# Scores by four 64x64 matmuls side by side, in two bursts per batch, for batches 2 to 7

## The chip, the cores and the metric

The kernel runs on one core of one Trainium2 chip. A core has a matrix engine (TensorE, in the profile PE, its weight loads PEld), VectorE (DVE), ScalarE (ACT), GpSimd (POOL) and a queue engine (SyncE, SP), which work through their own instruction streams in order and wait for each other by semaphores. The metric is the device time of one execution in microseconds (us). Less is better.

## The reference

Sliding-window causal attention over 8 batches and 8 heads, followed by two dense layers with a gate between them:

```python
B, H, S, D = 8, 8, 576, 64                    # q, k, v: [B, H, S, D] float32
scores = q @ k.T / sqrt(D)                    # per batch and head
scores = where((0 <= i - j) & (i - j < 64), scores, -1e9)
attn = softmax(scores)                        # over the keys
x = (attn @ v).transpose(0, 2, 1, 3).reshape(B * S, H * D)     # 4608 x 512
h = x @ w_in                                  # w_in 512 x 2048
out = (h * cos(h)) @ w_out                    # w_out 2048 x 512, out 4608 x 512 float32
```

A query sees only itself and the 63 keys before it. So the 576 rows of a batch and head fall into 9 blocks of 64 queries, and block j needs the keys of blocks j - 1 and j alone (block 0 only its own 64).

## The kernel before, in words

**Units and groups.** Heads are taken in four pairs p. A unit (b, p, j) is the scores of one pair and one query block: 128 rows (64 queries of each of the two heads) by 128 keys. Up to four units make a group, which shares one PSUM bank and goes as one through the softmax: `g_scores` (TensorE), `g_max` (VectorE: mask, scale and row minimum of the negative, out of PSUM), `g_exp` (ScalarE, one exponential per unit), `g_inv` (VectorE reciprocal), `g_norm` (the product with it, on GpSimd, for one group of batch 2 on VectorE) and `g_trans` (a transposing DMA from the SP queue, which makes the weights wT). `CUTS` lists, batch by batch, which query blocks form the groups and in which order: batch 2 takes blocks 0 to 5 of all pairs first, batch 3 blocks 0 to 4, the others 0 to 3.

**Scores of batches 2 to 7.** q stands in SBUF in a padded form `qB`: for each pair and block a 128x128 tile with head 0's 64x64 in one corner, head 1's in the opposite one, and zeros (memsets `ms.0` to `ms.7` in the list `FIRST`) in the others. One 128x128 matmul per unit (line 303) then gives both heads' scores. q gets there by TensorE transposes (`tr_q`, line 219) and two half copies by VectorE (`put_block`), or, for the chunks counted in `TURNED`, by a transposing DMA (`turn_q`) and VectorE copies (`put_turned`). k is turned by transposing DMAs in six chunks (`turn_k`).

**Values and the dense layers.** 4608 rows make nine tiles mt of 512 rows (8 blocks each, while a batch has 9, so tile mt starts in batch mt - 1 and ends in batch mt for mt from 2 to 7). Per tile: `values` (line 384, attention times v, pair after pair, 16 matmuls each), `put_x` (copies to xT; the one of pair 2 by ScalarE), 64 matmuls h_ps (line 453) with a sine by ScalarE and a product by VectorE behind each four, and 64 matmuls out_ps (line 609).

**What sets the order.** Each engine's stream is written out by hand: up to tile 1 by the list `FIRST`, then by planned times. `at(time, step)` puts a step on a plan, `pump(time)` issues all that is due; one tile is T = 32 units of planned time, 16 for h_ps and 16 for out_ps. The scores of batch b are issued in tile b - 1 from planned time 14.6 on, a group after each few out_ps matmuls (`PACE`), each later step of a group by its lag (`LAGS`: 0.2, 1, 3, 3.2, 3.8). In the same tile GpSimd copies half of batch b's v rows to the other half of the partitions (`spread_v`, two copies at planned time 24 for batch 3 and 22.2 for later ones; for batch 2 a DMA does it at 10), and issues the loads. The values of tile b are planned at the end of tile b - 1. PSUM has eight banks: five named ones (O0, O1, X0, X1, S), which h_ps, out_ps and scores share, and three in a rotating pool `ps_t` (tag "t"), which the transposes of q and the values use.

**Batches 0 and 1** are scored by 64x64 matmuls, one per head, the two of a pair on opposite quarters of TensorE's array (line 309).

Of the kernel before, what the change touches and what calls it, by code (L numbers as in the profile page):

```python
# [10 lines left out]
def _safe_warn(msg, *a, **kw):  # L11
# [12 lines left out]
NU = 9  # L24
NC, NP = 6, 96
GF = 4
LAST = 384
PACE = 0.36
CUTS = (
# [6 lines left out]
)  # L36
# [39 lines left out]
def kernel(  # L76
# [28 lines left out]
    first_q = moe.tile([128, 2, d_model], F32, tag="out", name="qT", bufs=OUTS).rearrange("p a f -> p (a f)").bitcast(BF16)  # L105
    qtiles = [first_q[:, S * i:S * i + S] for i in range(PAIRS - 1)]
    qtiles.append(const.tile([128, S], BF16, name="qT3"))
    turned = const.tile([128, PAIRS, S], BF16, name="qT")
    qtiles += [turned[:, p] for p in range(PAIRS)]
    qsets = [const.tile([128, PAIRS, NU, 2, 64], BF16, name=f"qB{i}") for i in range(2)]  # L110
    qblocks = [qset[:, p] for qset in qsets for p in range(PAIRS)]
# [16 lines left out]
    S_BANKS = ("X1", "S", "X0")  # L128
# [146 lines left out]
    for b, cuts in enumerate(CUTS, 2):  # L275
        for cut in cuts:
            for p0 in range(0, PAIRS, 2):
                for of, lo, hi in cut:
                    groups += [[(b, p, j) for p in range(p, p + of) for j in range(lo, hi)] for p in range(p0, p0 + 2, of)]
    direct = set(range(n_first)) | {n_first + i for i in DIRECT}  # L280

    def g_scores(n, which):
        s_ps = bank((BANKS if n < n_listed else S_BANKS)[which], "s_ps")
# [12 lines left out]
        for u, (b, p, j) in enumerate(units):  # L296
            kt = st["kT", b, p]
            lo, chunks = max(64 * j - 64, 0), 2 if j else 1
            rhs = kt[:, lo:lo + 64 * chunks].rearrange("d (a t) -> d a t", a=chunks)
            if j and j % 2 == 0:  # L300
                rhs = rhs[:, ::-1, :]
            if b > 1:
                nc.tensor.matmul(out=s_ps[:, u, 0:64 * chunks].rearrange("p (a t) -> p a t", a=chunks),  # L303
                                 lhsT=qblocks[(b % 2) * PAIRS + p][:, j].rearrange("d h t -> d (h t)"), rhs=rhs,
                                 start=True, stop=True, skip_group_check=True)
                continue
            for h in range(2):
                d = slice(64 * h, 64 * h + 64)
                nc.tensor.matmul(out=s_ps[d, u, 0:64 * chunks].rearrange("p (a t) -> p a t", a=chunks),  # L309
                                 lhsT=qtiles[b * PAIRS + p][d, 64 * j:64 * j + 64], rhs=rhs[d], start=n >= n_first,  # L310
                                 stop=n >= n_first or u == len(units) - 1, skip_group_check=True)
# [3 lines left out]
    def g_max(n):  # L315
# [4 lines left out]
        else:  # L320
            s = att.tile([128, GF, 128], F32, tag="s", name="s", bufs=4)
            for u, (b, p, j) in enumerate(units):
# [7 lines left out]
    def g_exp(n):  # L330
# [3 lines left out]
        for u, (_, _, j) in enumerate(groups[n]):  # L334
# [5 lines left out]
    def g_inv(n):  # L340
        e, den = st["e", n]
        for u, (_, _, j) in enumerate(groups[n]):
# [13 lines left out]

    def g_trans(n):
# [10 lines left out]
        st.update({("wT", unit): wT[:, i] for i, unit in enumerate(groups[n])})  # L368

    def g_put(n, engine=None):  # L370
        wT, u = att.tile([128, GF, 128], BF16, tag="wT", name="wT", bufs=20), len(groups[n])
        copy(engine, wT[:, 0:u], st.pop(("tw", n))[:, 0:u])
        st.update({("wT", unit): wT[:, i] for i, unit in enumerate(groups[n])})


    def values(mt, p, lo=0, hi=TU):
# [3 lines left out]
        for i in range(lo, hi):  # L380
            b, j = divmod(mt * TU + i, NU)
            wT = st["wT", (b, p, j)]
            for h in range(2):
                nc.tensor.matmul(out=o_ps[64 * h:64 * h + 64, 64 * i:64 * i + 64],  # L384
                                 lhsT=vtiles[b % 2][:, max(j - 1, 0), 128 * p + 64 * h:128 * p + 64 * h + 64],
                                 rhs=wT[:, 64 * h:64 * h + 64], start=True, stop=True, skip_group_check=True)
# [9 lines left out]
    def values_half(a, g):  # L396
        st["o", a, g] = o_ps = ps_t.tile([128, 2, half], F32, tag="t", name="o_ps")
        for p in (0, 1):
            for i in range(GF):
                j = GF * g + i  # L400
                wT = st["wT", (0, 2 * a + p, j)]
                for h in range(2):
                    nc.tensor.matmul(out=o_ps[64 * h:64 * h + 64, p, 64 * i:64 * i + 64],
                                     lhsT=vtiles[0][:, max(j - 1, 0), 128 * (2 * a + p) + 64 * h:128 * (2 * a + p) + 64 * h + 64],
                                     rhs=wT[:, 64 * h:64 * h + 64], start=True, stop=True, skip_group_check=True)
# [81 lines left out]
    ready = {(0, p, j): 0 for p in range(PAIRS) for j in range(TU)}  # L487
    ready.update({unit: 0 for units in groups[:n_listed] for unit in units})
    n = n_listed
    for t in range(1, B - 1):  # L490
        last = max(i for i, units in enumerate(groups) if units[0][0] == t + 1)
        time = T * t + Q - 1.4
        for i in range(last + 1 - n):
            time += PACE * len(groups[n - 1]) if i else 0
            at(time, g_scores, n, i % 3)
            lags = LAGS[:2] + tuple(T * t + T - 0.79 - time + 0.01 * s for s in range(3)) if n == last else LAGS
# [3 lines left out]
            at(time + (4.6 if n in direct else lags[-1]), g_trans, n)  # L500
            if n in direct:
                at(time + 4.9, g_put, n)
            ready.update({unit: time + (5.9 if n in direct else 8.5) for unit in groups[n]})
            n += 1

    for b in range(2, B):
        t0 = T * (b - 1)
        for h in range(2):
            if b in TURNED:
                at(t0 + 0.6 + 0.5 * h, put_turned, b, h, 0, 3)  # L510
            if TURNED.get(b, 0) > 2:
                at(t0 + (11 + h if TURNED[b] == NC else 10 + 0.5 * h), put_turned, b, h, 3, TURNED[b] * NP // 64)
        for c in range(TURNED.get(b, 0)):
            at(t0 - T + (24.3 if b == 4 else 23.4 if c < 2 else 26.4) + 0.01 * c, turn_q, b, c)
        for p in range(PAIRS if TURNED.get(b) != NC else 0):
            t_q = t0 + (2 if b == 2 else 1) + (3.3 if b == 2 else 3.5) * p
            for lag, fn, *args in ((0, tr_q), (0.02, put_block, 0), (0.5, put_block, 1)):
                at(t_q + lag, fn, b, p, *args)
# [130 lines left out]
```

## Time and profile before

| | us |
|---|---|
| Time, median of 3 runs (lowest to highest) | 310.14 (308.4 to 311.36) |
| Profiled execution: span from first to last instruction | 306.3 |
| Profiled execution: its own time | the page gives the span alone |
| TensorE busy (matmuls) | 296.2 |
| ScalarE busy | 234.3 |
| VectorE busy | 228.5 |
| GpSimd busy | 192.5 |

Everything in the page and the trace counts from the span's start; between the span and the time of a run lie 3.8 us by the median. The busy time of an engine is an average over stages: h_ps and out_ps alternate, and the softmax runs beside out_ps. The chain of waits names, piece by piece in order of time, the work that ended last; the timeline names each instruction of one engine; DMA answers give the us from issue to landing.

### The profile page before, as it was taken

The numbers are of one execution on the slowest core, as the hardware profiler recorded it, in microseconds if no ns is written. First come the engines' busy times: TensorE is split into PE (matmuls) and PEld (weight loads), VectorE is DVE, ScalarE is ACT, GpSimd is POOL, SyncE is SP. The second block draws the span as 40 slices with busy tenths as digits, with TensorE's granted clock in tenths as the row PEclk, the third lists the DMA queues.
The fourth block names the chain that finished last, engine by engine and source line by source line (L and its number), as shares of the span: only waits on it lengthen the run. The fifth ranks groups of instructions, "written<-read, shape, count | busy, mean of one in ns | idle before, by whom it ended". The sixth has DMA issues, their size and how long they took to land.

```text
span 306.3 us, 7904 instructions
## 1 busy us (share of the span) xinstructions
PE 296.2 (97%) x2616; PEld 159.0 (52%) x2616; DVE 228.5 (75%) x908; ACT 234.3 (76%) x785; POOL 192.5 (63%) x228
## 2 busy tenths in 40 slices
PE   3889999999999999999999999999999999999996
PEld 2768844545555555445544555454545554454443
DVE  5999978599769976798579857986698668235801
ACT  5998799677997799779976997699879986116600
POOL 8998579995659669967998599959903930000000
PEclk9999999999999999999999999999999999999999
DMA  7999999999999995999999999999794643011011
GB/s 146 179 212 192 200 180 130 121 149 191 226 113 116 175 223 80 121 133 232 125 121 137 231 143 104 157 221 148 86 137 107 169 78 141 2 68 71 1 67 70
DMA packets 159945, 42.14 MB, mean 138 GB/s; under 512 B 148256, under 2 KB 155168, under 8 KB 159904
## 3 DMA queue, kind: packets, MB, share of 16 engines
q0 software_dynamic: 100192, 18.06, 80.1%
q1 hardware_dynamic: 59568, 23.38, 40.6%
q8 instruction: 20, 0.33, 0.4%
q14 instruction: 21, 0.17, 0.2%
q10 hardware_dynamic: 144, 0.20, 0.2%
HBM read 36.70 MB, written 9.44 MB: 151 GB/s over the span
## 4 chain that ended last, share of the span: by engine, by line
PE 90%; POOL 4%; DMA 2%; DVE 1%; ACT 1%; issue 1%; POOLq 0%; DVEq 0%; ACTq 0%
PE h_ps L453 35%; PE out_ps L609 35%; PE h_ps L417 5%; PE s_ps L303 4%; PE out_ps L436 4%; PE o_ps L384 3%; DMA k<-in_k_dram 2%; POOL w L353 2%; PE tq_ps L219 1%; POOL v L188 1%; PE out_ps L465 1%; PE s_ps L309 1%; PE tw_ps L364 1%; POOL w_in L204 1%; ACT e L336 1%
## 5 line engine op out<-in xcount | busy, mean ns | idle before, releaser
L609 PE MATMUL out_ps<-w_out,gT 128*128 128x512 bf16 x496 | 117.3, 379 | 0.0
L453 PE MATMUL h_ps<-xT,w_in 128*128 128x512 bf16 x512 | 115.3, 379 | 0.3
L595 ACT ACTIVATE sin<-h_ps 128x512 f32<-128x512 f32 x128 | 73.7, 598 | 32.7 <-PE h_ps L453 31.4
L598 DVE TENSOR_TENSOR gT<-h_ps,sin 128x512 bf16<-128x512 f32 x128 | 82.1, 685 | 21.9 <-ACT sin L595 21.2
L336 ACT ACTIVATE e<-s,negm 128x128 f32<-128x128 f32 (+1 forms) x256 | 97.1, 382 | 0.6 <-DVE negm L324 0.6
L353 POOL TENSOR_TENSOR w<-e,rden 128x512 bf16<-128x512 f32 (+1 forms) x74 | 70.0, 962 | 36.6 <-DVE rden L346 18.8
L453 PEld LDWEIGHTS <-w_in 128*128 128x128 bf16 x512 | 48.8, 98 | 54.7 <-issue 0.4
L609 PEld LDWEIGHTS <-gT 128*128 128x128 bf16 x496 | 45.9, 98 | 44.2
L324 DVE CUSTOM_DVE_ANT_0 s<-s_ps,mask 128x128 f32<-128x128 f32 (+1 forms) x256 | 56.4, 279 | 1.7 <-PE s_ps L309 0.9
L336 ACT ACTIVATION_READ_ACCUMULATOR e<-s,negm 128x1 f32 x256 | 48.3, 189 | 0.0
L182 POOL DMA_DIRECT2D q<-in_q_dram x36 | 28.3, 785 | 10.7 <-DMA q<-in_q_dram 4.0
L188 POOL DMA_DIRECT2D v<-in_v_dram x40 | 34.4, 878 | 0.3 <-issue 0.2
L182 POOL DMA_DIRECT2D k<-in_k_dram x36 | 28.2, 783 | 3.9 <-DMA k<-in_k_dram 1.2
L137 ACT COPY out_sb<-out_ps 128x512 f32<-128x512 f32 (+1 forms) x18 | 10.2, 566 | 24.5 <-PE out_ps L609 18.4
L346 DVE RECIPROCAL rden<-den 128x4 f32<-128x4 f32 (+1 forms) x79 | 13.1, 166 | 19.0 <-ACT e L336 18.6
L303 PEld LDWEIGHTS <-qB 128*128 128x128 bf16 x216 | 16.5, 98 | 14.2
L137 DVE CAST xT<-o_ps 128x512 bf16<-128x512 f32 x24 | 15.5, 677 | 10.1 <-PE o_ps L384 10.1
L137 DVE COPY out_sb<-out_ps 128x512 f32<-128x512 f32 x18 | 12.4, 690 | 13.2 <-PE out_ps L609 12.5
L324 DVE DVE_READ_ACCUMULATOR2_ANT negm<- 128x1 f32 x256 | 21.3, 83 | 0.0
L303 PE MATMUL s_ps<-kT,qB 128*128 128x128 bf16 (+1 forms) x216 | 21.2, 216 | 0.0
L137 POOL COPY v<-v 64x1536 bf16<-64x1536 bf16 (+3 forms) x12 | 18.8, 1570 | 0.3
L137 DVE COPY qB<-tq_ps 64x384 bf16<-64x384 bf16 (+1 forms) x40 | 15.6, 390 | 0.4
(70 smaller groups left out, 257.8 us busy)
## 6 DMA issues: line engine op xcount, KB each, us to landing
out_dram<-out_sb SPq DMA_DIRECT2D x16, 512.0 KB, 7.5
v<-in_v_dram POOLq DMA_DIRECT2D x32, 128.0 KB, 5.7
q<-in_q_dram POOLq DMA_DIRECT2D x36, 96.0 KB, 8.6
k<-in_k_dram POOLq DMA_DIRECT2D x36, 96.0 KB, 8.5
w_in<-in_moe_w_in_dram POOLq DMA_DIRECT2D x4, 512.0 KB, 8.7
w_out<-in_moe_w_out_dram POOLq DMA_DIRECT2D x4, 512.0 KB, 10.8
wT<-w SPq DMA_TRANSPOSE x68, 4.4
q<-in_q_dram POOLq DMA_DIRECT2D x7, 144.0 KB, 6.0
```

What stands on the lines that cost most here:

```text
L137: {"a": nc.scalar.copy, "p": nc.gpsimd.tensor_copy}.get(engine, nc.vector.tensor_copy)(out, in_)
L182: nc.gpsimd.dma_start(out=st[name, b][:, c].rearrange("p (h d) -> p h d", h=H), in_=src.rearrange("h p d -> p h d"))
L188: nc.gpsimd.dma_start(out=vt.rearrange("p (h d) -> p h d", h=H), in_=v[b, :, c * 128:c * 128 + n, :].rearrange("h p d -> p h d"))
L303: nc.tensor.matmul(out=s_ps[:, u, 0:64 * chunks].rearrange("p (a t) -> p a t", a=chunks), lhsT=qblocks[(b % 2) * PAIRS + p][:, j].rearrang ...
L324: nc.vector.tensor_tensor_reduce(out=s[:, u, c], in0=s_ps[:, u, c], in1=mask[:, 2 - j % 2 if j else 0, c], scale=-scale if b else -1.0, sc ...
L336: nc.scalar.activation(e[:, u, c], s[:, u, c], AF.Exp, bias=negm[:, u:u + 1], scale=1.0 if n < n_first else -1.0, accum_out=den[:, u:u + 1])
L353: (nc.gpsimd if engine == "p" else nc.vector).tensor_tensor(out=w[:, 0:u], in0=e[:, 0:u], op=ALU.mult, in1=rden[:, 0:u].unsqueeze(2).to_br ...
L417: nc.tensor.matmul(out=h_ps[:, half * e:half * e + half], lhsT=w_in_sb[:, ks, ff * 128:ff * 128 + 128], rhs=st["xT", 0][:, ks, half * g:ha ...
L453: nc.tensor.matmul(out=st["h", ff], lhsT=w_in_sb[:, ks, ff * 128:ff * 128 + 128], rhs=st["xT", mt][:, ks], start=start, stop=stop)
L595: nc.scalar.activation(sin, h_ps, AF.Sin, bias=math.pi / 2.0)
L598: nc.vector.tensor_tensor(out=gt[:, e], in0=h_ps, in1=sin, op=ALU.mult)
L609: nc.tensor.matmul(out=o_ps[e], lhsT=gT[ff // 2][:, ff % 2, ms * 128:ms * 128 + 128], rhs=w_out_sb[:, ff], start=ff == 0, stop=ff == n_ff - 1)
```

## The change

For batches 2 to 7 the padded q is given up. q is held once per pair (`qsets`, two buffers of 128 x 4 x 576, taken in turn by even and odd batches; batches 0 and 1 use them too); TensorE's transposes are copied out by one copy of all 128 partitions, and the turning DMA writes into it without a copy behind it. The memsets go.

The scores are taken in two bursts per batch, at planned times 14.6 (query blocks 0 to 3, four banks: X1 and three of the rotating pool) and 20.6 (blocks 4 to 8, five banks: S, X0, X1 and two of the pool). A group now holds two neighbouring blocks of all four pairs, for one head of each pair: its unit (b, a, j, h) is head h of pairs 2a and 2a + 1, on the two halves of the 128 rows. Two groups, one for each h, are filled together, so that four 64x64 matmuls in a row use the four quarters of the array, two into each of two banks. Block 8 forms a ninth group of the old kind. The later steps of group n of a batch are planned at 14.6 + 1.6 n and the same lags. `wT` is kept by head. Nine groups per batch take the place of ten to twelve; the `s` buffers go from four to six. Batches 0 and 1 are scored as before.

```diff
-PACE = 0.36
-CUTS = (
-    (((1, 0, 4), (2, 4, 6)), ((1, 6, 9),)),
-    (((1, 0, 3), (2, 3, 5)), ((1, 5, 9),)),
-    (((1, 0, 4),), ((1, 4, 7), (2, 7, 9))),
...
-)
+PACE = 1.6
+BURSTS = ((0, 4, ("X1", "t", "t", "t")), (4, 8, ("S", "X0", "X1", "t", "t")))
+BURST = (14.6, 20.6)
...
-    qsets = [const.tile([128, PAIRS, NU, 2, 64], BF16, name=f"qB{i}") for i in range(2)]
-    qblocks = [qset[:, p] for qset in qsets for p in range(PAIRS)]
+    qsets = [const.tile([128, PAIRS, S], BF16, name=f"qT{i}") for i in range(2)]
...
     def put_q(b, p, engine=None):
-        of, to = in_order(st.pop(("tq", b, p)), qtiles[b * PAIRS + p], b)
+        if b > 1:
+            lo = TURNED.get(b, 0) * NP
+            copy(engine, qsets[b % 2][:, p, lo:], st.pop(("tq", b, p))[:, lo:])
+            return
+        of, to = in_order(st.pop(("tq", b, p)), qsets[b][:, p], b)
...
-    def put_block(b, p, h):
-        d = slice(64 * h, 64 * h + 64)
-        lo = TURNED.get(b, 0) * NP // 64
-        copy("d", qblocks[(b % 2) * PAIRS + p][d, lo:, h], st["tq", b, p][d].rearrange("d (j t) -> d j t", j=NU)[:, lo:])
-
     def turn_q(b, c):
-        nc.sync.dma_start(out=turned[:, :, c * NP:c * NP + NP], in_=st["q", b][:, c], transpose=True)
-
-    def put_turned(b, h, lo, hi):
-        d = slice(64 * h, 64 * h + 64)
-        copy("d", qsets[b % 2][d, :, lo:hi, h], turned[d].rearrange("d a (j t) -> d a j t", j=NU)[:, :, lo:hi])
+        nc.sync.dma_start(out=qsets[b % 2][:, :, c * NP:c * NP + NP], in_=st["q", b][:, c], transpose=True)
...
-    for b, cuts in enumerate(CUTS, 2):
-        for cut in cuts:
-            for p0 in range(0, PAIRS, 2):
-                for of, lo, hi in cut:
-                    groups += [[(b, p, j) for p in range(p, p + of) for j in range(lo, hi)] for p in range(p0, p0 + 2, of)]
+    bursts = []
+    for b in range(2, B):
+        for lo, hi, banks in BURSTS:
+            bursts.append((b, len(groups), banks))
+            for j in range(lo, hi, 2):
+                groups += [[(b, a, j + e, h) for e in range(2) for a in range(2)] for h in range(2)]
+        groups.append([(b, p, NU - 1) for p in range(PAIRS)])
...
+    def burst_scores(n):
+        b, g0, banks = bursts[n]
+        for g, which in enumerate(banks, g0):
+            s_ps = ps_t.tile([128, MT], F32, tag="t", name="s_ps") if which == "t" else bank(which, "s_ps")
+            st["s", g] = s_ps.rearrange("p (u c) -> p u c", c=128)
+        for g in range(g0, g0 + len(banks), 2):
+            for u in range(GF):
+                for n in range(g, min(g + 2, g0 + len(banks))):
+                    _, p, j, *h = groups[n][u]
+                    for e in range(2):
+                        pe, he = (2 * p + e, h[0]) if h else (p, e)
+                        d = slice(64 * he, 64 * he + 64)
+                        rhs, chunks = keys(b, pe, j)
+                        to = st["s", n][64 * e:64 * e + 64, u, 0:64 * chunks]
+                        nc.tensor.matmul(out=to.rearrange("p (a t) -> p a t", a=chunks),
+                                         lhsT=qsets[b % 2][d, pe, 64 * j:64 * j + 64], rhs=rhs[d], start=True, stop=True,
+                                         skip_group_check=True)
...
-            if b > 1:
-                nc.tensor.matmul(out=s_ps[:, u, 0:64 * chunks].rearrange("p (a t) -> p a t", a=chunks),
-                                 lhsT=qblocks[(b % 2) * PAIRS + p][:, j].rearrange("d h t -> d (h t)"), rhs=rhs,
-                                 start=True, stop=True, skip_group_check=True)
-                continue
...
+    def put_wT(n, wT):
+        for i, (b, p, j, *h) in enumerate(groups[n]):
+            for e in range(2):
+                st["wT", (b, 2 * p + e, j, h[0]) if h else (b, p, j, e)] = wT[:, i, 64 * e:64 * e + 64]
...
-                                 rhs=wT[:, 64 * h:64 * h + 64], start=True, stop=True, skip_group_check=True)
+                                 rhs=st["wT", (b, p, j, h)], start=True, stop=True, skip_group_check=True)
...
+    for i, (b, g0, banks) in enumerate(bursts):
+        t = T * (b - 1)
+        at(t + BURST[i % 2], burst_scores, i)
+        for n in range(g0, g0 + len(banks)):
+            time = t + BURST[0] + PACE * (n - bursts[i - i % 2][1])
+            lags = LAGS[:2] + tuple(t + T - 0.79 - time + 0.01 * s for s in range(3)) if n == bursts[i | 1][1] + 4 else LAGS
             for lag, fn in zip(lags, (g_max, g_exp, g_inv)):
                 at(time + lag, fn, n)
             at(time + lags[3], g_norm, n, "d" if n == n_listed + 5 else "p")
-            at(time + (4.6 if n in direct else lags[-1]), g_trans, n)
...
+            at(time + lags[4], g_trans, n)
...
-    def clear_first(p, engine):
-        (nc.gpsimd if engine == "p" else nc.vector).memset(qblocks[p].rearrange("d j h t -> d (j h t)"), 0.0)
```

More of the change, by code (lines that the diff above doesn't have):

```diff
@@ L296, in g_scores @@
         for u, (b, p, j) in enumerate(units):
[L297 to L301, printed above, removed]
-            if b > 1:
-                nc.tensor.matmul(out=s_ps[:, u, 0:64 * chunks].rearrange("p (a t) -> p a t", a=chunks),
-                                 lhsT=qblocks[(b % 2) * PAIRS + p][:, j].rearrange("d h t -> d (h t)"), rhs=rhs,
-                                 start=True, stop=True, skip_group_check=True)
-                continue
+            rhs, chunks = keys(b, p, j)
             for h in range(2):
@@ L333, in g_exp @@
         den = att.tile([128, GF], F32, tag="den", name="den", bufs=8)
-        for u, (_, _, j) in enumerate(groups[n]):
+        for u, (_, _, j, *_) in enumerate(groups[n]):
             c = slice(0, 128 if j or n < n_first else 64)
@@ L341, in g_inv @@
         e, den = st["e", n]
-        for u, (_, _, j) in enumerate(groups[n]):
+        for u, (_, _, j, *_) in enumerate(groups[n]):
             if j == 0 and n >= n_first:
@@ L367, in g_trans @@
         nc.sync.dma_start(out=wT[:, 0:u], in_=w[:, 0:u].rearrange("p u c -> p (u c)"), transpose=True)
-        st.update({("wT", unit): wT[:, i] for i, unit in enumerate(groups[n])})
+        put_wT(n, wT)
     def g_put(n, engine=None):
@@ L372, in g_put @@
         copy(engine, wT[:, 0:u], st.pop(("tw", n))[:, 0:u])
-        st.update({("wT", unit): wT[:, i] for i, unit in enumerate(groups[n])})
+        put_wT(n, wT)
     def values(mt, p, lo=0, hi=TU):
```

47 lines of the change are left out of this document (12 added, 35 removed), and 13 rows, old and new, of tables (CUTS, FIRST).

## The prediction, made before the changed kernel had run

> **What bounds the kernel now.** I read the page's engine totals first, then the chain of waits, then the table by stage.
>
> ```profile
> PE 296.2 (97%) x2616; PEld 159.0 (52%) x2616; DVE 228.5 (75%) x908; ACT 234.3 (76%) x785; POOL 192.5 (63%) x228
> PE 90%; POOL 4%; DMA 2%; DVE 1%; ACT 1%; issue 1%; POOLq 0%; DVEq 0%; ACTq 0%
> core 0: us, PE busy (x) PEld busy (x) DVE busy (x) ACT busy (x) POOL busy (x), PEclk, DMA share, GB/s
> 135.88:152.76 16.88, 16.85 (x166) 9.09 (x162) 12.82 (x92) 16.81 (x78) 13.97 (x15) 1.00 1.55 179
> 152.76:167.40 14.64, 14.64 (x83) 7.06 (x83) 12.65 (x27) 10.27 (x17) 13.16 (x17) 1.00 1.93 124
> ```
>
> TensorE carries 90% of the chain at clock 1.00, so an edit is worth the TensorE time it removes, as long as no wait moves in. The two stretches are one period. In the second (h_ps) every other engine has slack. In the first (scores, out_ps, values) ScalarE is busy for 16.81 of 16.88 us: the weights of a batch come out at the pace of the exponentials, whatever TensorE does. The chain of waits of that stretch, when batch 4 is scored:
>
> ```profile
> 135.88 0.20 PE s_ps L303 x4
> 136.08 1.73 PE out_ps L609 x8
> ...
> 148.15 3.45 PE out_ps L609 x16
> 151.60 1.13 PE o_ps L384 x64
> 152.73 0.03 issue
> 152.76 2.75 PE h_ps L453 x12
> ```
>
> From 135.88 to 151.60 are 15.72 us. The 64 out_ps matmuls take 64 x 3.45/16 = 13.80, so the scores take 1.92 us a batch, 11.5 us in six batches. Nothing else stands there.
>
> **The change, part by part.** Scores. Per batch, 36 matmuls of 128x128 become 72 of 64x64: a burst of 32 and one of 40. Batch 1 of this kernel already runs 64x64 matmuls, two side by side:
>
> ```profile
> 40.04 0.48 PE s_ps L309 x14
> 40.53 1.83 PE out_ps L436 x8
> 42.36 0.34 PE s_ps L309 x8
> 37.14 0.57 PE tq_ps L216 x36
> ```
>
> Fourteen against eight are three more pairs, one of them 64 columns wide, for 0.14 us: 0.056 for a full pair, 0.028 for the short one, as much as one full-size score matmul. Eight in 0.34 leave 0.34 - 4 x 0.056 = 0.12 for leaving the shape, and out_ps behind a burst costs 1.83 where eight otherwise cost 1.73 (row at 136.08): 0.10 more. A burst has a fixed price of 0.22.
>
> What no row shows is four tiles at once. Below, a set of four cannot beat 0.056 (one pair); above, it costs 0.111 (two pairs in turn). The nearest rows say how fast small matmuls with their weight loads can follow: 36 in 0.57 are 0.016 each, 0.063 a set. I take 0.056, since two pairs on different quarters need what one pair needs, and keep 0.111 for the range. Burst one: 6 sets at 0.056, 2 short ones (row block 0 sees 64 keys) at 0.028, 0.22: 0.61. Burst two: 8 sets, 4 pairs for row block 8, 0.22: 0.89. Sum 1.50, 0.42 less per batch, 2.5 us in six.
>
> [...]
>
> Padding gone. Eight memsets, the doubled q copies and the copies out of the turned q leave VectorE, all in stretches where TensorE waits for other things or for nothing:
>
> ```profile
> L546 DVE MEMSET qB<- 128x576 uint32 x8 | 4.3, 538 | 0.6
> 14.51 4.09 POOL w L353 x4
> ```
>
> The start hangs on loads and then on GpSimd's four products at 14.51, so I credit 0. Should VectorE's freed time pull the first products forward, that is 0.1 at most: GpSimd issues loads until 14.31.
>
> ScalarE. Same 36 exponentials, starting behind the same table load, so their ends stay. With TensorE 0.42 ahead, xT's third part is what could be late next:
>
> ```profile
> 152.52 0.59 ACT L137 CAST xT<-o_ps 128x512 bf16<-128x512 f32 x1
> ```
>
> It is ready at 152.52 + 0.59 = 153.11. TensorE wants it after six h_ps matmuls, 152.76 + 1.30 = 154.06, then 153.64. It still fits.
>
> The order of the weights. This is where the gain can be lost. Before, a group held one or two pairs, and the cuts put the row blocks that the next values step needs into the first groups. Now group 2i and 2i+1 of a batch hold row blocks 2i, 2i+1 of all pairs, one head each, so pair 0, the first of the values step, needs the last needed group already. A group's weights pass exponentials, reciprocal, GpSimd's product (one wait in GpSimd's queue holds all behind it), SP's transposing DMA. The v copy of each batch (two pieces) stands in GpSimd's queue too; its planned time is unchanged (24 for batch 3, 22.2 later), the products' times are not. In the built order it now stands ahead of products 4 and 5 in batch 3 (before: behind the sixth of the old groups, the last needed) and ahead of product 3 in batches 4 and 5 (before: behind the fourth).
>
> Batch 3 (values need blocks 0 to 4, so groups 0 to 5):
>
> ```profile
> 106.40 0.33 ACT L336 ACTIVATE e<-s,negm 128x64 f32<-128x64 f32 x1
> 106.73 0.39 ACT L336 ACTIVATE e<-s,negm 128x128 f32<-128x128 f32 x1
> 114.32 1.04 POOL L353 TENSOR_TENSOR w<-e,rden 128x512 bf16<-128x512 f32 x1 [0.67 <-POOL w L353]
> 115.30 3.40 POOL L137 COPY v<-v 64x1536 bf16<-64x1536 bf16 x2
> 118.79 3.03 POOL L353 TENSOR_TENSOR w<-e,rden 128x512 bf16<-128x512 f32 x3
> 120.11 1.23 SPq L367 DMA_TRANSPOSE wT<-w  x1
> wT<-w SPq DMA_TRANSPOSE x1, 2.5
> 120.05 1.13 PE o_ps L384 x64
> 121.21 2.75 PE h_ps L453 x12
> ```
>
> Group 3 ends its exponentials at 106.40 + 4 x 0.33 + 12 x 0.39 = 112.4; its product runs 112.6 to 113.6; the copy occupies GpSimd for 118.79 - 115.30 = 3.49, to 117.0; products 4 and 5 end at 118.0 and 119.0. The second's transpose starts on SP behind the first's (1.23 each, from 118.05), at 119.3, and lands 2.5 later, like the one issued at 120.11: 121.8. TensorE would reach the matmul that needs it (the last of pair 0's eight blocks) at 120.05 - 0.42 + 0.3 = 119.9. It stands for 1.9 us; then some 0.95 of the step is left, and h_ps starts at 122.7, not 121.21: +1.5.
>
> Batch 2 (blocks 0 to 5, six groups; no GpSimd copy, the last product on VectorE):
>
> ```profile
> 84.87 0.69 DVE L353 TENSOR_TENSOR w<-e,rden 128x512 bf16<-128x512 f32 x1
> wT<-w SPq DMA_TRANSPOSE x1, 3.0
> 88.16 1.13 PE o_ps L384 x64
> 89.32 2.75 PE h_ps L453 x12
> ```
>
> Product done at 85.56, landed 3.0 later at 88.6. Before, pairs 2 and 3 alone needed it, last. Now pair 0 does at 88.16 - 0.42 + 0.3 = 88.0: a stand of 0.6, and h_ps at 88.6 + 1.0 = 89.6: +0.3.
>
> Batches 4 and 5 (group 3 behind the copy):
>
> ```profile
> 140.59 3.23 POOL L353 TENSOR_TENSOR w<-e,rden 128x512 bf16<-128x512 f32 x3
> qT<-q SPq DMA_TRANSPOSE x1, 4.3
> 174.38 1.04 POOL L353 TENSOR_TENSOR w<-e,rden 128x512 bf16<-128x512 f32 x1 [0.47 <-DVE rden L346]
> qT<-q SPq DMA_TRANSPOSE x1, 3.9
> 183.15 1.13 PE o_ps L384 x64
> ```
>
> Third products end at 143.8 and 175.4; plus 3.49 and a product of 1.04, the transposes start at 148.3 and 179.9. Landing takes 2.4 (quiet) to 4.3 and 3.9 (the transposes issued at 147.3 and 179.6): 150.7 to 152.6, and 182.3 to 183.8. They are needed at 151.4 and 182.9. In the middle they come with a stand of about 0.1: -0.3 each (ends -0.42 and +0.8). Batches 6 and 7 need only groups 0 and 1: -0.42 each.
>
> Sum: 0.3 + 1.5 - 0.3 - 0.3 - 0.42 - 0.42 = +0.4 us. The page gives the profiled execution its span alone, 306.3; the median of the runs is 310.1, 3.8 above, which I carry over: 306.7, so 310.5.
>
> **The rivals.** All weights arrive in time (GpSimd or the landings faster than I set them): six times -0.42, 307.6. Against it stands the queue order; for it only that batch 2 kept its deadline. Four do not run side by side, the change doing half of what it says: 16 sets at 0.111 (two short ones at 0.056), 2.33 a batch, +0.41; it decides as soon as a set costs more than about 0.08. Batch 3 still ends by its weights (+1.5), the other five pay 0.41: +3.5, 313.6, slower. For it: no row shows two head halves writing the same rows of two banks. Against: pairs cost the same as one. [...] Keys late: burst two needs the last key chunk at its planned time 20.6, all at once. In batch 5:
>
> ```profile
> 167.43 0.20 PE s_ps L303 x4
> 165.15 2.21 SPq L260 DMA_TRANSPOSE kT<-k  x1
> kT<-k SPq DMA_TRANSPOSE x1, 8.2
> ```
>
> It lands at 173.3, and TensorE asks at 167.43 + 0.61 + 6 x 0.86 + 0.4 = 173.6. A slip of 1 in two batches makes +2, less what hides batch 5's weights: 312.
>
> **How the numbers follow.** The forecast has 0.50, all in time 0.17, keys late 0.13, not side by side 0.15, else 0.05. The range runs from the second to the fourth with what the runs scatter: 307.8 to 313.7. About 1%, 3.1 us, is what a measurement of this kernel can tell from no change. Faster by more needs the best case and a little: 0.06. Slower by more: the pairs, part of the keys and the rest, 0.22. Within: 0.72.
>
> **What would show it.** In the profile after: 72 score matmuls a batch with starts a few ns apart in fours, about 0.6 and 0.9 us per burst; a hole of TensorE near 2 us in the values step of batch 3, released by a wT transpose, 0.6 in batch 2's, hardly one later; periods 0.42 shorter for batches 6 and 7. I am wrong if a set takes 0.1, if holes stand ahead of burst two, or if GpSimd's products 4 and 5 of batch 3 end before 118.

## The result, and the profile after

The changed kernel takes 314.72 us as the median of 20 runs (310.68 to 318.27), beside 309.39 us for the kernel before (20 runs, 308.38 to 311.36). The ratio is **1.0123, with a 95% interval of 1.0096 to 1.0150**: slower, by 3.8 us of 309.4. (The ratio is formed without runs that lie more than 1.5% above the fastest of their kernel; over all runs the medians differ by 5.3 us, and the section on the clock tells where most of the rest comes from.) The forecast was 310.5 us, +0.4, in a range of 307.8 to 313.7: 1.0123 times 309.4 are 313.2, inside it, and the median of all runs lies above it. By the bound of 1% the change is slower, which had a chance of 0.22.

The profiled execution took 312.69 us, its span 310.9. First the totals of the engines and the shares of the chain, from the page:

```profile
PE 292.3 (94%) x2800; PEld 153.9 (49%) x2832; DVE 215.6 (69%) x864; ACT 234.9 (76%) x785; POOL 191.4 (62%) x222
PE 75%; DMA 9%; POOL 4%; ACT 3%; SPq 3%; issue 2%; DVE 2%; POOLq 0%; DVEq 0%; ACTq 0%
```

TensorE is busy for 3.9 us less than before (296.2), but that figure is too large to be the saving: 32 of its matmuls have no record here (2800 against 2832 weight loads), and the second profile of the kernel before, which lacks 32 as well, shows 1.9 us less than the first without any edit. What the change saves is read from an undisturbed stage, below. TensorE's share of the chain fell from 90% to 75%, and DMA's rose from 2% to 9%: TensorE now waits for transfers. Such a wait of TensorE is called a stand from here on. Where it waits, the summary of TensorE's waits between 60 and 252 us tells (what it waited for, us in total, times, the longest):

```profile
PE s_ps L285 <- DMA kT<-k: 2.4, 3, 1.5
PE o_ps L386 <- DMA wT<-w: 1.9, 2, 1.1
PE out_ps L594 <- issue: 1.7, 11, 0.2
```

The last line is no wait: it is a missing out_ps record behind a burst. The first is the keys, the second the weights. Which batch they hit is read from the table by stage, cut at the first h_ps of each stage (the stretch, its length, busy time of each engine, the granted clock):

```profile
core 0: us, PE busy (x) PEld busy (x) DVE busy (x) ACT busy (x) POOL busy (x), PEclk, DMA share, GB/s
57.93:89.91 31.98, 31.48 (x290) 15.69 (x290) 24.99 (x119) 28.00 (x101) 22.20 (x27) 1.00 1.85 173
89.91:123.61 33.70, 31.41 (x284) 15.79 (x288) 23.95 (x111) 27.71 (x97) 25.95 (x28) 1.00 1.46 144
123.61:154.78 31.17, 30.73 (x276) 15.27 (x281) 23.66 (x111) 26.93 (x94) 25.91 (x28) 1.00 1.47 141
154.78:188.51 33.73, 31.41 (x277) 15.53 (x281) 23.77 (x111) 27.78 (x96) 25.97 (x28) 1.00 1.61 150
188.51:219.68 31.17, 30.72 (x276) 15.25 (x281) 23.66 (x111) 26.71 (x94) 25.92 (x28) 1.00 1.79 149
219.68:250.99 31.31, 30.33 (x261) 14.66 (x264) 22.83 (x107) 27.60 (x96) 16.69 (x16) 1.00 0.98 133
```

The same cut of every profile of this study gives the lengths of the stages in which batches 2 to 7 are scored. The first column is the time of the first such h_ps, the last is the end of the last matmul:

| kernel | start | batch 2 | 3 | 4 | 5 | 6 | 7 | end |
|---|---|---|---|---|---|---|---|---|
| before | 57.17 | 32.15 | 31.89 | 31.55 | 31.55 | 31.55 | 30.85 | 303.39 |
| before, again | 58.14 | 32.15 | 31.89 | 31.55 | 31.55 | 31.55 | 30.85 | 304.36 |
| the change | 57.93 | 31.98 | 33.71 | 31.17 | 33.72 | 31.17 | 31.31 | 307.68 |
| v copy early | 58.01 | 31.97 | 35.66 | 33.16 | 31.21 | 31.43 | 30.51 | 308.65 |
| burst two later | 57.98 | 33.29 | 34.15 | 32.18 | 32.82 | 31.17 | 31.38 | 309.66 |
| pairs in turn | 57.75 | 32.07 | 33.71 | 32.91 | 33.85 | 31.23 | 31.26 | 309.47 |
| v copy on VectorE | 59.13 | 32.03 | 34.09 | 31.17 | 31.28 | 31.17 | 30.51 | 306.07 |
| and q turned late | 58.10 | 31.77 | 31.75 | 31.17 | 31.98 | 31.17 | 30.51 | 303.15 |
| before, late weights | 59.27 | 32.16 | 34.55 | 33.25 | 31.55 | 31.54 | 30.85 | 309.86 |
| halves in turn | 59.79 | 32.43 | 33.71 | 31.68 | 33.35 | 31.67 | 31.45 | 310.77 |
| and the last weights late | 57.79 | 31.80 | 31.55 | 31.17 | 31.21 | 31.17 | 30.51 | 301.90 |

For the change, against the kernel before, this gives -0.17, +1.82, -0.38, +2.17, -0.38 and +0.46: 3.5 us, and 0.76 more at the start. Batches 4 and 6 show what the scores themselves bring, batches 3, 5 and 7 what is lost.

The undisturbed stage, batch 4, answers the lines from which the prediction took the scores (chain of waits of the changed kernel):

```profile
138.28 0.52 PE s_ps L285 x32
138.81 0.16 issue
138.97 5.13 PE out_ps L594 x23
144.09 0.80 PE s_ps L285 x40
144.89 0.16 issue
145.05 8.58 PE out_ps L594 x39
153.63 1.13 PE o_ps L386 x64
```

Two bursts stand where ten small groups stood, and no wait is between them and the values. In the trace the four matmuls of a set start 3 to 4 ns apart, and full sets follow each other 0.056 us apart. From the last 512-column matmul ahead of a burst to the first on record behind it are 1.06 and 1.33 us (137.906 to 138.966, 143.714 to 145.046); without two steps of 0.216, one of them for the missing record, the bursts cost 0.63 and 0.90 us.

Batch 3, the same view:

```profile
118.84 1.33 POOL w L351 x2
120.17 2.43 DMA wT<-w
122.60 0.04 issue
122.64 0.95 PE o_ps L386 x49
```

and GpSimd in the same stretch, in order of time (start, length, instruction, how often):

```profile
113.35 1.04 POOL L351 TENSOR_TENSOR w<-e,rden 128x512 bf16<-128x512 f32 x1 [0.50 <-POOL w L351]
114.33 3.40 POOL L124 COPY v<-v 64x1536 bf16<-64x1536 bf16 x2
117.82 4.03 POOL L351 TENSOR_TENSOR w<-e,rden 128x512 bf16<-128x512 f32 x4
```

The v copy stands ahead of products 4 and 5, product 5 ends near 119.9, its transpose is issued at 120.17 and lands at 122.60, and TensorE, which stood for 0.75 and 1.10 us, does its last 49 value matmuls in 0.95. SP was not far from being the last link itself: it turned two chunks of q (issued at 115.71 and 117.01) behind the transpose of group 3, was free at 118.21, and issued that of group 4 at 118.89, when its product was done. In the kernel before, the same two turns stood behind six transposes of weights.

Batch 5 loses at another place, ahead of the scores. TensorE in order of time:

```profile
175.30 0.42 PE L285 MATMUL s_ps<-kT,qT 64*64 64x128 bf16 x16
175.97 0.31 PE L285 MATMUL s_ps<-kT,qT 64*64 64x128 bf16 x8 [0.26 <-DMA kT<-k]
177.78 0.53 PE L285 MATMUL s_ps<-kT,qT 64*64 64x128 bf16 x16 [1.50 <-DMA kT<-k]
```

The keys come late because SP issued them late. SP's queue of the changed kernel from 145 us:

```profile
151.95 3.56 SPq L230 DMA_TRANSPOSE qT<-q  x2
155.61 2.54 SPq L370 DMA_TRANSPOSE wT<-w  x2
158.25 2.61 SPq L242 DMA_TRANSPOSE kT<-k  x2
...
169.18 1.26 SPq L242 DMA_TRANSPOSE kT<-k  x1
```

The same for the kernel before:

```profile
147.22 3.38 SPq L244 DMA_TRANSPOSE qT<-q  x2
150.70 3.81 SPq L367 DMA_TRANSPOSE wT<-w  x3
154.60 2.51 SPq L260 DMA_TRANSPOSE kT<-k  x2
...
165.15 2.21 SPq L260 DMA_TRANSPOSE kT<-k  x1
```

The last chunk of keys goes out at 169.18 instead of 165.15, 4.0 us later, of which the stage itself accounts for 2.0 (154.78 against 152.76, from batch 3). The other 2.0 come with the turn of q, at 151.95 against 147.22: it waits in SP's queue behind the transpose of group 3 (issued at 150.66), and that waits for the first of the products behind the v copy. GpSimd of the changed kernel, in order of time:

```profile
146.11 3.41 POOL L124 COPY v<-v 64x1536 bf16<-64x1536 bf16 x2
149.59 4.03 POOL L351 TENSOR_TENSOR w<-e,rden 128x512 bf16<-128x512 f32 x4
```

### The profile page after: what moved, and what is told of

It is laid out like the page before. It is cut to its first block, busy times and chain, and to the rows that moved or that the text cites. A ratio compares the mean times of both kernels' runs of the same rounds, so it can differ in the third digit from the quotient of the medians.

```text
span 310.9 us, 8217 instructions
## 1 busy us (share of the span) xinstructions
PE 292.3 (94%) x2800; PEld 153.9 (49%) x2832; DVE 215.6 (69%) x864; ACT 234.9 (76%) x785; POOL 191.4 (62%) x222
## 4 chain that ended last, share of the span: by engine, by line
PE 75%; DMA 9%; POOL 4%; ACT 3%; SPq 3%; issue 2%; DVE 2%; POOLq 0%; DVEq 0%; ACTq 0%
PE h_ps L454 32%; PE out_ps L594 27%; PE h_ps L418 4%; DMA w_in<-in_moe_w_in_dram 3%; PE out_ps L437 3%; PE o_ps L386 3%; DMA wT<-w 3%; SPq L242 2%; ACT e L334 2%; PE s_ps L285 2%; DMA q<-in_q_dram 2%; PE tq_ps L206 1%; POOL w L351 1%; POOL v L175 1%; PE out_ps L466 1%
## 5 line engine op out<-in xcount | busy, mean ns | idle before, releaser
L594 PE MATMUL out_ps<-w_out,gT 128*128 128x512 bf16 x482 | 106.8, 379 | 2.0 <-issue 1.9
L583 DVE TENSOR_TENSOR gT<-h_ps,sin 128x512 bf16<-128x512 f32 x128 | 85.0, 688 | 29.1 <-ACT sin L580 28.5
L351 POOL TENSOR_TENSOR w<-e,rden 128x512 bf16<-128x512 f32 (+1 forms) x68 | 69.1, 1031 | 41.2 <-DVE rden L344 38.7
L454 PEld LDWEIGHTS <-w_in 128*128 128x128 bf16 x512 | 48.8, 98 | 54.8 <-issue 0.4
L594 PEld LDWEIGHTS <-gT 128*128 128x128 bf16 x496 | 47.5, 98 | 56.6
L344 DVE RECIPROCAL rden<-den 128x4 f32<-128x4 f32 (+1 forms) x73 | 12.3, 168 | 23.5 <-ACT e L334 23.2
L124 DVE COPY out_sb<-out_ps 128x512 f32<-128x512 f32 x18 | 12.4, 688 | 13.2 <-PE out_ps L594 12.4
L437 PE MATMUL out_ps<-w_out,gT 128*128 128x512 bf16 x60 | 15.1, 380 | 0.4 <-issue 0.3
L418 PE MATMUL h_ps<-xT,w_in 128*128 128x256 bf16 x128 | 14.6, 273 | 0.5 <-DMA w_in<-in_moe_w_in_dram 0.5
L418 PEld LDWEIGHTS <-w_in 128*128 128x128 bf16 x128 | 12.3, 98 | 2.2 <-DMA w_in<-in_moe_w_in_dram 0.7
```

Source lines behind the costliest of these rows:

```text
L124: {"a": nc.scalar.copy, "p": nc.gpsimd.tensor_copy}.get(engine, nc.vector.tensor_copy)(out, in_)
L351: (nc.gpsimd if engine == "p" else nc.vector).tensor_tensor(out=w[:, 0:u], in0=e[:, 0:u], op=ALU.mult, in1=rden[:, 0:u].unsqueeze(2).to_br ...
L418: nc.tensor.matmul(out=h_ps[:, half * e:half * e + half], lhsT=w_in_sb[:, ks, ff * 128:ff * 128 + 128], rhs=st["xT", 0][:, ks, half * g:ha ...
L437: nc.tensor.matmul(out=st["out", m], lhsT=st["g", ff // 2][:, ff % 2, m * 128:m * 128 + 128], rhs=w_out_sb[:, ff], start=ff == 0, stop=ff ...
L454: nc.tensor.matmul(out=st["h", ff], lhsT=w_in_sb[:, ks, ff * 128:ff * 128 + 128], rhs=st["xT", mt][:, ks], start=start, stop=stop)
L583: nc.vector.tensor_tensor(out=gt[:, e], in0=h_ps, in1=sin, op=ALU.mult)
```

## The experiments

The theory after the result (A): scores are 0.38 us a batch cheaper, and the loss is the order of two queues, GpSimd's (the v copy ahead of products) and SP's behind it, which carries the weights of this batch and the keys of the next. The rivals: burst two simply asks for the last keys too early (B); or the loss is not in the stands at all, but in a later start and a lower clock.

### The kernel before, once more

No edit.

> The kernel before, once more, for what its own runs scatter: when the first h_ps of stage 1 starts (57.17 us in its first profile, 57.93 with the change) and the mean granted clock of each run. If the later start and the clock below 1.00 belong to the change, this run shows 57.2 within 0.1 and a clock of 1.000 in every run. If they are scatter, it shows starts up to 57.9 and some runs at 0.99. Ratio to before 1.000 within 0.003.

309.19 us (10 runs), ratio 0.9997 (0.9966 to 1.0028). Its start is at 58.14, 0.97 later than in its first profile, and all its stages have the same length to 0.01 us. So the 0.76 at the start of the change lies within the scatter and is put down to no edit: in the table above the kernel before and its variant with late weights start at 57.17 to 59.27, the change and its variants at 57.75 to 59.79. The mean clock was 0.999 or 1.000 in all ten runs; of the 55 further runs of the kernel before that went beside the experiments, 3 were below 0.997.

### The v copy early, on GpSimd

```diff
-at(t0 + ((24 if b == 3 else 22.2) + 0.1 * half_ if b > 2 else 10), spread_v, b, half_, "p" if b > 2 else "s")
+at(t0 + ((22.2 if b == B - 1 else 15) + 0.1 * half_ if b > 2 else 10), spread_v, b, half_, "p" if b > 2 else "s")
```

> The change, with GpSimd's v copy of batches 3 to 6 planned at 15 instead of 24 (batch 3) and 22.2, behind the last load that GpSimd issues and ahead of all the products of the batch. Theory A (the copy in GpSimd's queue holds the products, SP's transposes behind them, and with those the keys of the next batch): the stand of 1.85 us in the values of batch 3 goes, and of the stands of batch 5 (2.0 at burst two, 0.3 at the values) and batch 7 (0.7) most goes: 4 us less than the change, a ratio to before of 0.995 to 1.002. Theory B (burst two asks for the last keys too early, whatever GpSimd does): only batch 3 gains, batches 5 and 7 keep their 2.0 and 0.7: a ratio of about 1.006. If the loss is the clock or the start, the ratio stays above 1.008 though the holes go.

314.42 us (6 runs), ratio 1.0150 (1.0107 to 1.0192). One half of theory A held: batches 5 and 7 lost their stands (31.21 and 30.51), though burst two stayed where it was, which theory B excludes. The other half fell: batch 3 stood longer, not shorter. TensorE in order of time:

```profile
120.27 0.41 PE L386 MATMUL o_ps<-wT,v 128*64 128x64 bf16 x14
122.93 0.21 PE L386 MATMUL o_ps<-wT,v 128*64 128x64 bf16 x1 [2.24 <-DMA wT<-w]
124.22 1.50 PE L386 MATMUL o_ps<-wT,v 128*64 128x64 bf16 x49 [1.08 <-DMA wT<-w]
```

and SP's queue of this run:

```profile
112.22 5.52 SPq L370 DMA_TRANSPOSE wT<-w  x4
117.84 2.50 SPq L230 DMA_TRANSPOSE qT<-q  x2
120.43 2.52 SPq L370 DMA_TRANSPOSE wT<-w  x2
```

The copy now holds the first product instead of the fifth, so the first transpose is issued at 112.22 instead of 109.91; from there SP issues eight transposes without a pause, 1.3 us each, and whatever the first is late the last is late. Two of the eight turn q for batch 4 and stand ahead of the two weights that batch 3 still needs. In this run SP, not GpSimd, is the last queue in batch 3. And batch 4 grew by 2.0 us without a stand: see the section on the clock.

### Burst two later

```diff
-BURST = (14.6, 20.6)
+BURST = (14.6, 22.6)
...
-            time = t + BURST[0] + PACE * (n - bursts[i - i % 2][1])
+            time = max(t + BURST[0] + PACE * (n - bursts[i - i % 2][1]), t + BURST[i % 2])
```

> The change, with burst two of each batch planned at 22.6 instead of 20.6, two blocks of out_ps (1.72 us) later, and its groups' maxima no earlier than that. Theory A: batch 3 keeps its 1.85, batch 5 keeps 2.0 - 1.72 = 0.3 of its stand and batch 7 none: 2.4 us less than the change, if ScalarE can take it. Theory B: the same in batches 5 and 7, so this run and the one with the early v copy have to be read together. The rival to both: the groups of burst two come 1.7 later, ScalarE (16.81 of 16.88 us busy in that stretch before) stands for as long, and the last weights and xT come later: no gain, or up to 1.5 us more in each of six batches.

313.16 us (4 runs), ratio 1.0110 (1.0066 to 1.0155), the same as the change. The stands for keys at burst two are gone in batches 5 and 7 (a wait of 0.30 for keys is now ahead of burst one of batch 7), but the rival to both theories held as well: batch 2 went from 31.98 to 33.29, where late weights stop the values three times, and in batch 5 they do so for 0.29, 0.63 and 0.20 us (32.82). (The 32.18 of batch 4 have a mean clock of 0.97 in them.) The weights need the scores as early as they come. Moving the demand is no remedy; the order of the queues has to change.

### Four at once, or not: two orders within a burst

```diff
-            for u in range(GF):
-                for n in range(g, min(g + 2, g0 + len(banks))):
+            for n in range(g, min(g + 2, g0 + len(banks))):
+                for u in range(GF):
```

> The change, with the four matmuls of a set no longer next to each other: a group's eight matmuls (one head, so the same 64 rows of TensorE) run through before those of the other group of the pair of groups. If four tiles run at once and two of one row half only as two, a set of four takes 0.111 in the place of 0.056: bursts of 1.00 and 1.34 us instead of 0.61 and 0.89, 0.84 a batch, where batches 3 and 5 hide it in part behind their late data: 3.5 to 5 us more than the change. If order within a burst is of no account, because TensorE overlaps what it finds, both bursts keep their length and the time is the change's.

The burst kept its length, within 0.03 us, and batch 6 took 31.23 instead of 31.17: the second expectation. The time, 314.65 us (4 runs), ratio 1.0156 (1.0119 to 1.0193), has no more in its stages than the change but a slow stretch of the clock in batch 4. So the order of eight matmuls hardly matters. With a longer run of one half it does:

```diff
-        for g in range(g0, g0 + len(banks), 2):
-            for u in range(GF):
-                for n in range(g, min(g + 2, g0 + len(banks))):
+        for first in range(2):
+            for n in range(g0 + first, g0 + len(banks), 2):
+                for u in range(GF):
```

> The change, with the groups of one head half (64 rows of TensorE) all before those of the other within a burst: 16 matmuls on one row half, then 16 on the other. The run with pairs in turn kept the length of the burst. If TensorE works on both row halves at once only as far as a short queue for each reaches, this longer run of one half can't overlap, and burst one takes about 0.8 to 1.0 instead of 0.53 from its first start to the first out_ps. If a pair on one row half costs 0.028 by itself, the burst keeps 0.53.

Burst one of batch 4 in the change, with pairs in turn, and with halves in turn (one line each, of three kernels):

```profile
138.22 0.59 PE L285 MATMUL s_ps<-kT,qT 64*64 64x64 bf16 x32
```

```profile
139.82 0.62 PE L285 MATMUL s_ps<-kT,qT 64*64 64x64 bf16 x32
```

```profile
140.54 0.79 PE L285 MATMUL s_ps<-kT,qT 64*64 64x64 bf16 x32
```

Burst two goes from 0.86 to 1.16 in the last, and batch 6 from 31.17 to 31.67. Running the two row halves at once is worth 0.50 us a batch, less than the 0.83 that the prediction's 0.111 for two pairs in turn would give, since the halves still overlap where one ends and the other begins: the second half's first pair starts at 140.744, between pairs of the first, whose last starts at 140.902. So burst one takes 0.73 us from its first start to the first out_ps, more than the 0.53 of one expectation and less than the 0.8 to 1.0 of the other. With the halves in turn the change would lose 0.12 us a batch instead of gaining 0.38. So matmuls for the two halves ran side by side where they came in turns of eight or fewer (0.62 and 0.59 us for 32 of them); in turns of sixteen only a part of them did (0.79). (One run, 315.76 us: no verdict on its time.)

### The v copy on VectorE, then q turned later

```diff
-at(t0 + ((24 if b == 3 else 22.2) + 0.1 * half_ if b > 2 else 10), spread_v, b, half_, "p" if b > 2 else "s")
+early = 2 < b < B - 1
+at(t0 + (18.6 + 1.6 * half_ if early else 22.2 + 0.1 * half_ if b > 2 else 10), spread_v, b, half_,
+   "d" if early else "p" if b > 2 else "s")
```

> The change, with the v copy of batches 3 to 6 on VectorE (its two pieces behind the maxima of groups 2 and 3) instead of GpSimd. GpSimd's products then follow the exponentials. Theory A, as the early copy left it (GpSimd's copy holds the products; behind it SP, at 1.3 us a transpose, is the next queue): batches 5 and 7 lose their stands as with the early copy (periods near 31.2 and 30.5). In batch 3 product 5 ends near 118.0, as with the early copy, but SP still turns two chunks of q between the transposes of groups 3 and 4: group 5 is issued near 119.6 and lands near 122.0, a stand of 1.4 against 1.85. Time 2 to 3 us under the change, a ratio to before of 1.000 to 1.005. If GpSimd alone was to blame, batch 3 has no stand at all and the ratio is 0.995.

311.79 us (10 runs), ratio 1.0072 (1.0046 to 1.0098). Batches 5 and 7 are clean (31.28, 30.51), as with the early copy, and here no slow stretch of the clock in batch 4 has a part in it. The last keys for batch 5 go out 12.7 us behind the start of their stage (169.13 against 156.42), where the change took 14.4 and the kernel before 12.4. Batch 3 stood for 1.12 and 1.12 us, more than the 1.4 expected: the copies, 0.67 and 0.88 us on VectorE, stand there ahead of the reciprocals of groups 1 and 2, for which GpSimd's products waited 1.16 and 0.89 us. But the order of the reasons is as expected: GpSimd's copy is out of the way, and SP still turns q first (two turns from 117.90, the last two weights only at 120.49). So the copy on GpSimd is not the whole cause of the stand in batch 3.

```diff
-            at(t0 - T + (24.3 if b == 4 else 23.4 if c < 2 else 26.4) + 0.01 * c, turn_q, b, c)
+            at(t0 - T + (26.5 if b == 4 else 23.4 if c < 2 else 26.4) + 0.01 * c, turn_q, b, c)
```

> As the run before, and the two chunks of q that SP turns during batch 3 planned behind the transpose of group 5 (26.5 instead of 24.3). Theory A with SP as the second queue: the stand in batch 3 falls to 0.5 or less, no stand of TensorE is over 0.5 us, the granted clock is 1.00 in every run, and the periods are those of the change without stands: 31.98, 31.6, 31.2, 31.2, 31.2, 30.5. Against the periods of before (32.15, 31.89, 31.55, 31.55, 31.55, 30.85) 1.9 us less: 307.5, a ratio of 0.994. If the stand in batch 3 stays, the exponentials set it, and the ratio is as in the run before.

308.43 us (12 runs), ratio 0.9983 (0.9956 to 1.0011). Two DMA issues moved behind the two weights that batch 3 still needs took 2.3 us out of it (34.09 to 31.75). Whether this move alone would do, with the copy left on GpSimd, was not run. SP's queue of this run:

```profile
109.90 9.49 SPq L370 DMA_TRANSPOSE wT<-w  x6
119.49 1.20 SPq L230 DMA_TRANSPOSE qT<-q  x1
```

Six weights in a row, and no stand in the values. What is left is in batch 5 (31.98): the summary of TensorE's waits has two lines, each once:

```profile
PE s_ps L285 <- DMA kT<-k: 0.2, 1, 0.2
PE o_ps L386 <- DMA wT<-w: 0.2, 1, 0.2
```

The ratio was 0.994 by the expectation; batch 5 is most of the difference. A clock of 1.00 in every run was expected too, and one of the 12 shows 0.994.

### The last weights behind the keys

```diff
-            at(time + lags[4], g_trans, n)
+            at(t + T - 0.3 + 0.01 * n if n >= bursts[i | 1][1] + 2 else time + lags[4], g_trans, n)
...
-at(t0 + (18.6 + 1.6 * half_ if early else 22.2 + 0.1 * half_ if b > 2 else 10), spread_v, b, half_,
+at(t0 + (24.5 + 1.6 * half_ if early else 22.2 + 0.1 * half_ if b > 2 else 10), spread_v, b, half_,
```

> The run with the v copy on VectorE and q turned late, with two more moves: the transposes of groups 6 to 8 of a batch, which no values step of that batch needs, go on SP behind all the keys of the next batch, and the v copy stands behind the maxima of group 6. If SP's order is what is left of the loss in batch 5 (0.24 of a hole at burst two for keys, 0.19 at the values, 0.8 in the period), the last keys are issued some 3 us sooner, both holes go, the period of batch 5 comes to 31.2, and the time is 0.8 us under that run: a ratio to before of 0.995 to 0.997. If the loads of k or the landing of the transposes set it, the period stays at 32.0 and the ratio at 0.998.

307.75 us (12 runs), **ratio 0.9936 (0.9903 to 0.9969)**: 0.6% faster than the kernel before, by an interval that excludes 1, and a little more than expected. All stands are gone, batch 5 takes 31.21, and the summary of TensorE's waits has nothing left but the missing records. SP now issues the six key chunks for batch 5 in a row (152.62 to 160.42). The two moves were made together, so what each is worth by itself is open. Against the kernel before the six stages are 0.35, 0.34, 0.38, 0.34, 0.38 and 0.34 us shorter, 2.1 us together: this is the gain of the bursts once no queue takes it back, as in batches 4 and 6 of the change. The mean clock was below 0.997 in 1 of 12 runs.

### The clock: a stand in the kernel before

In the run with the early v copy, batch 4 grew without a stand. The table by stage of that run, behind the end of batch 3's long stand:

```profile
123.00:126.00 3.00, 1.92 (x51) 1.54 (x51) 1.53 (x4) 0.35 (x1) 0.08 (x1) 0.50 0.53 106
126.00:129.00 3.00, 2.78 (x7) 1.06 (x7) 0.45 (x1) 1.51 (x2) 3.00 (x4) 0.50 0.30 53
```

The granted clock is 0.50 behind the stand, and an h_ps matmul takes 0.427 us instead of 0.216 from start to start. Whether the stand alone does this, or the 64x64 bursts have a part in it, a stand in the kernel before shows:

```diff
-            at(time + (4.6 if n in direct else lags[-1]), g_trans, n)
+            at(time + (4.6 if n in direct else lags[-1] + (1.6 if n == n_listed + 15 else 0)), g_trans, n)
```

> The kernel before, with one transposing DMA moved on SP: that of the last weights which the values of batch 3 need goes behind the two turns of q and the next weights, so it is issued near 121.4 and lands near 123.9, and TensorE stands for 3.0 us in the values of batch 3. No 64x64 scores here. If a stand alone halves the granted clock, the 4 to 6 us behind it show 0.5 to 0.6 and the time rises by 3.0 and another 2 to 3: 314 to 315, mean clock 0.99. If the 64x64 bursts were needed for it, the clock stays 1.00 and the time is 312.3.

313.94 us (4 runs), ratio 1.0116 (1.0077 to 1.0155). TensorE in order of time, and a row of the table by stage:

```profile
125.73 0.32 PE L384 MATMUL o_ps<-wT,v 128*64 128x64 bf16 x8 [2.57 <-DMA wT<-w]
125.98 4.45 PE L453 MATMUL h_ps<-xT,w_in 128*128 128x512 bf16 x12
```

```profile
126.00:129.00 3.00, 3.00 (x12) 1.11 (x10) 0.69 (x1) 1.87 (x2) 3.00 (x4) 0.57 1.10 117
```

A stand of 2.57 us, without a single 64x64 score in that stage, lowers the clock too, to 0.57 in this row: batch 3 costs 2.66 more and batch 4, in which nothing else changed, 1.70. Three of its four runs had a mean clock of 0.995 or less. So the stand is enough.

Not every stand does it. The profiled execution of the change stood for 0.75 and 1.10 us in batch 3 and kept 1.00; the run with pairs in turn stood for 0.70 and 1.11 at the same place and fell to 0.57 between 123.5 and 127.5. Of the 20 runs of the change 11 had a mean clock below 0.997, with a median of 315.5 us, and 9 had not, with 313.0; among the 12 that form the ratio the medians are 314.7 and 313.0. This is most of why its runs spread so far and why its median lies higher than its profile, though not all: one run at 0.999 took 317.04. The runs without long stands (the last two of the queue experiments) were below 0.997 in 1 of 12 each. Of all runs with a clock on record, 28 of 48 of the kernels whose profile has stands of 1.8 us or more in batch 3 were below 0.997, and 5 of 90 of the others.

## Why the prediction was right, and where it was wrong

The forecast held that a saving in the scores is lost again in the queues, and that is what happened; but it held the two to cancel (+0.4), and the loss is the larger by 3.5 us in the stages of the profile, 3.8 by the ratio. That 313.2 lies in the range is in part luck: the range reaches up to 313.7 because of the rival in which the four matmuls do not run side by side, and the runs refute that rival. The rival that did come true, late keys, was priced at 312. By its own steps:

- **Scores, -0.42 a batch.** Right. The bursts cost 0.63 and 0.90 us against 0.61 and 0.89 forecast, and the undisturbed batches 4 and 6 gain 0.38. A set of four costs what a pair costs (0.056), and 32 matmuls in 0.59 are 0.018 each: the rival of 0.111 a set is refuted.
- **Memsets and copies, 0.** Not contradicted: the start differs by 0.76, and the kernel before differs from itself by 0.97, so a tenth could not be seen.
- **ScalarE and xT.** Right: batch 4 has no wait between the values and h_ps.
- **Batch 3, a stand of 1.9 and +1.5.** Right in place and size: 1.85, and +1.82. The forecast ended product 5 at 119.0; it ended near 119.9. Of the cause it had one half: GpSimd's copy was the last link in this kernel, as forecast, but the two turns of q, which SP now takes ahead of the transposes of groups 4 and 5, are in no step of the forecast. Without the copy they would have been the last link, 0.68 us sooner; with the copy moved to VectorE a stand of 2.24 was left, and it went only when the turns went behind the weights.
- **Batch 2, +0.3.** The size was off: the stand was 0.18 instead of 0.6, and the stage gained 0.17.
- **Batch 4, -0.3.** Right, -0.38. **Batch 6, -0.42:** -0.38.
- **Batch 5, -0.3, and batch 7, -0.42.** Wrong: +2.17 and +0.46, together 3.35 above their terms, where the whole sum is off by 3.1. The step that failed was the keys: the landing of the last chunk, 173.3, was taken from the trace of before as if SP would issue it when it did before. But the same v copy whose 3.49 us the prediction set ahead of product 3 holds that product's transpose on SP, and SP's queue holds the turns of q and the keys behind it. The early v copy and the copy on VectorE show it: the stands for keys go when the copy leaves its place, while burst two stays. The prediction followed the copy to the weights and stopped there; it named the late keys as a rival (0.13) and gave them a slip of 1 in two batches, where they slipped by 1.76 and 0.60.
- **The clock** was in no term. In 11 of 20 runs it is below 0.997, and these take 1.7 to 2.5 us more by their medians; the experiment that adds a stand to the kernel before shows that a stand can be the cause.

## What to carry to other kernels

When an instruction moves ahead of another in one queue, follow the wait through every queue that it feeds to its end: here one copy on GpSimd held a product, the product a transpose on SP, and that the keys of the next batch, and the last link cost most. Where a queue runs without a pause once it has begun, as SP's did here with eight transposes 1.3 us apart, a late first item makes the last one late, and it is the order within the queue, by when each result is needed, that helps: two turns of q moved behind two weights took 2.3 us out of batch 3. And price a stand of the matrix engine with the clock that it may cost behind it: here, in about half of the runs, 1.7 to 2.0 us on top of stands of 1.8 to 3.3.

## What the runs showed of the hardware

- **A short stand can halve TensorE's clock.** With the early v copy, stands of 2.24 and 1.08 us in the values of batch 3 went with a granted clock of 0.50 from 123 to 129 us. With pairs in turn it was 0.57 from 123.5 to 127.5, behind stands of 0.70 and 1.11, and 512-column matmuls started 0.427 apart instead of 0.216 from 124.26 to 127.25, with one step of 0.294 before and one of 0.347 behind them. In the kernel before, behind an added stand of 2.57, it was 0.57 from 126 to 129. It does not happen each time: 0.75 and 1.10 in the profile of the change, and 1.12 and 1.12 with the v copy on VectorE, left it at 1.00.
- **Pairs on one row half need not alternate one by one.** Eight matmuls of one half followed by eight of the other ran nearly as fast as the two mixed (0.62 against 0.59 us for 32 of them), sixteen and sixteen did not (0.79).
- **With the early v copy SP issued a transposing DMA every 1.3 us**, so eight of them were a queue of 10.7 us (112.22 to 122.95); in the profile of the change the time from issue to landing, 2.4 us on a quiet stretch (120.17 to 122.60), was 8.6 us for the last keys of batch 5, issued at 169.18 while GpSimd's loads ran.
